# The low part of the queries, taken one group earlier: top-32 attention and a routed feed-forward on one core

## The chip, the cores and the metric

The kernel runs on one core of a Trainium2 chip. The metric is the device time of one launch in microseconds (us); smaller is better. Five engines work side by side: PE multiplies matrices, DVE (VectorE) does the top-32 search, ACT (ScalarE) copies out of PSUM and takes exponentials, POOL (GpSimd) does elementwise side work, SP issues most transfers. Each engine works through its own instructions strictly in the order in which they were written.

## The reference, cut to what matters

```python
# 4 batches, 8 heads, 576 rows, head size 64
scores = q @ k.T / 8
kth = the 32nd largest of each row of scores
attn = softmax(where(scores >= kth, scores, -1e9))
x = attn @ v                       # heads side by side: 2304 tokens x 512
e = argmax(x @ w_gate + bias)      # one of 8 experts for each token
x = gate * (relu(x @ w1[e]) @ w2[e])
h = x @ w_in;  g = 0 below -1, (h + 1)^2 / 4 up to 1, h above
out = g @ w_out
```

The change touches the first stage alone. There the scores are wanted to about the exactness of f32, so q and k are each split into a high part, rounded to a shorter format, and a low part, the rest; three products (high x high, high x low, low x high) make the score.

## The kernel before

**Units and groups.** Heads go in pairs: 16 pairs `j`. One unit is 128 query rows against 576 keys; a pair has 9 units (8 with split products, the ninth, `u == 8`, from the unsplit tiles), so there are 144 units. Two units make a group `g`, 72 groups in all, and one pass of the loop in `attention` handles one group; a pair takes four and a half of them.

**One pass.** In pass `g` the engines are given, in this order: `topk(g)` for DVE (with POOL's part); the masks `w` of group g-1 (ACT, L295); the product with v of group g-2 (PE, L323); half of the scores of group g+4 (PE `qk`, L194 to L196; ACT `sevac`, L204); the turned probabilities of group g-1 (PE, L304 and L306; ACT L311); the first two entries of the list `bg`; the exponentials `e` of group g (ACT, L290); the other half of the scores of g+4; and the rest of `bg`. `bg` is `later[g]`, a list of side steps that `at(g, step, ...)` appends to in order.

**Even and odd passes of DVE.** `topk(g)` takes the eight largest of `lit2` (L251), of `lit` (L253) and of both together (L255), and then four rounds of replacing and searching (L267, L270). An odd pass has, behind L255, also the fold of the next *two* groups: `big`, `c` and `lit2` (L212, L213, L214). So odd passes are long and even ones short.

**What POOL does in a pass.** Two tiny copies of the group before (L240, `edge` and `top`); the factor `nm` (L256), once L255 is done; then `less(g + 1)`, two passes over 128x576 (L227, L233) that make the tile `lit` which DVE's L253 reads in the *next* pass. In an odd pass the first of the two also waits for the fold's end (L214; `add_manual_dep`, "shared port"). Behind these stand the side steps of `bg`: `krest` (the low part of the keys, L179, 128x576), `qrest` (the low part of the queries, L183, 128x512), and `xout` (the normalised output: two short steps on DVE, L344 and L345, then on POOL one product over 128x512, L348, and two over 64x64, L353).

**Where the side steps stand.** For each pair `prep(j, g)` is called with an odd `g`, a few passes before its first scores are due. `turn` transposes the keys or queries on PE (five transposes, L167) and copies them out twice on ACT: `kT` and `kh`, or `qT` and `qh` (L170, L175, L172). `xout` of an older pair is put at the head of the list of an odd pass, and it falls on the same odd passes as `qrest` for all but the first pairs.

Of the kernel before, what the change touches and what calls it, by code (L numbers as in the profile page):

```python
# [65 lines left out]
class Kernel:  # L66
# [32 lines left out]
    def attention(self, moe):  # L99
        nc, tc = self.nc, self.tc  # L100
        with ExitStack() as ctx:
# [264 lines left out]
            def at(g, f, *a):  # L366
                later.setdefault(max(g, 0), []).append((f, a))

            def odd(g):
                return g if g % 2 else g - 1  # L370

            def prep(j, g, *eng):

                at(g - 2, turn, j, "k")
                at(g - 2, krest, j, *eng)
                at(g - 1, turn, j, "q")
                at(g, qrest, j, *eng)

            load(0, nc.scalar)
            load_v(0, vtile(0))  # L380
            load(1)
            load_v(1, vtile(1))
            prep(0, 0, nc.vector)
            for g in range(4):
                for f, a in later.pop(g, []):
# [5 lines left out]
            for j in range(1, len(pairs)):  # L391
                g = odd((9 * j + 1) // 2 - AHEAD - 2)
                prep(j, g)
                if j + 1 < len(pairs):
                    at(g - 2, load, j + 1)
# [1328 lines left out]
```

## Time and profile before

| what | us |
|---|---|
| median of three runs | 1181.84 (1181.74 to 1182.97) |
| profiled execution, its own time | 1180.52 |
| its span in the trace | 1178.9 |
| busy: PE | 1109.3 (94%) |
| busy: DVE | 810.2 (69%) |
| busy: ACT | 709.8 (60%) |
| busy: POOL | 556.2 (47%) |

The shares are means over stages with different limits. Attention with the top-32 search takes about the first 490 us, the routing some 50 more, and the two feed-forward networks the rest. The change lies in the first stage alone, so that stage's own shares and waits are what counts. A wait in a row is the idle time of an engine just before an instruction, put down to the instruction that released it.

### The profile page before, as it was taken

How to read it: one execution, taken by the hardware profiler on the slowest of the kernel's cores; microseconds unless marked ns; L12 is line 12 of the kernel's file. 1: busy time of each engine (PE TensorE's matmuls, PEld its weight loads, DVE VectorE, ACT ScalarE, POOL GpSimd, SP SyncE). 2: the span in 40 equal slices, each digit the busy share in tenths (PEclk: the TensorE clock that was granted, in tenths of full speed). 3: DMA queues.
4: the chain of work that ended last, by engine and by line, in shares of the span. 5: the costliest groups of instructions: out<-in, count | busy, mean ns of one | idle time of the engine just before them, and what ended most of it. 6: DMA issues, size and time to landing. Idle time of an engine off the chain costs nothing. (4 is left out here: it accounts for less than half of the span.)

```text
span 1178.9 us, 24601 instructions
## 1 busy us (share of the span) xinstructions
PE 1109.3 (94%) x8900; PEld 944.4 (80%) x8901; DVE 810.2 (69%) x2523; ACT 709.8 (60%) x1262; POOL 556.2 (47%) x662
## 2 busy tenths in 40 slices
PE   8999899999998997887999999899999999999998
PEld 5777787877887885776888787778899999999897
DVE  6999999999999999887568889487332222323222
ACT  5989998999899985744554455254333333333322
POOL 2776777677677767622324455032322223232222
PEclk8989998999999997998999999999999999999999
DMA  4235573021111003366766565231101001010000
GB/s 88 55 114 176 185 233 119 15 45 44 25 27 37 12 13 126 108 205 212 239 198 214 187 224 179 78 130 54 54 1 37 19 1 54 1 55 1 27 1 28
DMA packets 120842, 106.66 MB, mean 90 GB/s; under 512 B 64384, under 2 KB 88960, under 8 KB 120704
## 3 DMA queue, kind: packets, MB, share of 16 engines
q1 hardware_dynamic: 116320, 94.67, 25.9%
q0 software_dynamic: 2880, 9.44, 2.4%
q8 instruction: 73, 1.20, 0.4%
q10 hardware_dynamic: 1504, 0.82, 0.2%
q14 instruction: 65, 0.53, 0.1%
HBM read 70.30 MB, written 34.60 MB: 89 GB/s over the span
## 5 line engine op out<-in xcount | busy, mean ns | idle before, releaser
L1206 POOL TENSOR_TENSOR gl<-g,gh 128x384 fp32r<-128x384 f32 x96 | 97.2, 1012 | 316.5 <-ACT gh L1205 289.5
L1200 ACT ACTIVATE c<-c,half 128x384 f32<-128x384 f32 x96 | 59.2, 617 | 161.9 <-DVE c L1199 157.1
L306 PE MATMUL tp<-nhuge,w 128*128 128x128 bf16 x720 | 137.1, 227 | 20.8 <-ACT w L295 20.5
L304 PE MATMUL tp<-ident,e 128*128 128x128 f32 x720 | 151.4, 297 | 0.5 <-issue 0.5
L1199 DVE TENSOR_SCALAR c<-h 128x384 f32<-128x384 f32 x95 | 52.8, 556 | 142.5 <-PE h L1057 140.1
L1054 PE MATMUL h<-xh,wih 128*128 128x384 f32 x380 | 130.5, 343 | 5.3 <-DVEq L1110 3.0
L1055 PE MATMUL h<-xh,wil 128*128 128x384 f32 x380 | 129.8, 341 | 0.0
L304 PEld LDWEIGHTS tp<-ident,e 128*128 128x128 f32 x720 | 105.4, 146 | 30.1 <-issue 11.2
L270 DVE MAX8 m<-z 128x8 f32<-128x160 f32 x432 | 117.5, 314 | 0.0
L1365 POOL TENSOR_TENSOR w1l<-w1r,w1h 128x512 fp32r<-128x512 f32 x41 | 57.7, 1408 | 124.7 <-ACT w1h L1364 98.4
L227 POOL TENSOR_TENSOR lit<-s 128x576 int32<-128x576 int32 x66 | 93.4, 1415 | 48.4 <-DVE lit L214 48.4
L1065 PE MATMUL y<-woh,gl 128*128 128x512 f32 x288 | 114.4, 397 | 1.5 <-POOL gl L1206 1.5
L1063 PE MATMUL y<-woh,gh 128*128 128x512 f32 x288 | 112.5, 391 | 1.7 <-ACT yo L1236 0.9
L1203 DVE TENSOR_TENSOR g<-c,h 128x384 f32<-128x384 f32 x95 | 52.6, 554 | 89.2 <-ACT c L1200 89.2
L1064 PE MATMUL y<-wol,gh 128*128 128x512 f32 x288 | 113.7, 395 | 0.0
L311 ACT ACTIVATE a<-tp 128x640 f32<-128x640 f32 x144 | 102.0, 708 | 18.9 <-PE tp L306 14.9
L295 ACT ACTIVATE w<-s,m 128x576 bf16<-128x576 f32 x144 | 103.6, 772 | 13.9 <-DVE m L270 13.9
L323 PE MATMUL tp<-v,a 128*64 128x65 f32 x2880 | 104.7, 228 | 2.1 <-issue 2.0
L323 PEld LDWEIGHTS tp<-v,a 128*64 128x64 f32 x2880 | 93.8, 141 | 15.5 <-issue 8.3
L290 ACT ACTIVATE e<-s,nm 128x576 f32<-128x576 f32 x144 | 103.5, 771 | 4.3 <-POOL nm L256 4.2
L306 PEld LDWEIGHTS <-w 128*128 128x128 bf16 x720 | 79.2, 111 | 26.9 <-ACT w L295 26.5
L204 ACT ACTIVATE s<-sp 128x576 f32<-128x576 f32 x144 | 92.8, 648 | 10.7 <-PE sp L196 9.1
(313 smaller groups left out, 2938.6 us busy)
## 6 DMA issues: line engine op xcount, KB each, us to landing
w1r<-in_moe_w_dram SPq DMA_DIRECT2D x56, 256.0 KB
w2r<-in_moe_w_dram SPq DMA_DIRECT2D x56, 256.0 KB
xs_dr<-zero SPq DMA_DIRECT2D x19, 512.0 KB
ys_dr<-zero SPq DMA_DIRECT2D x19, 512.0 KB
cr<-in_moe_w_in_dram SPq DMA_DIRECT2D x16, 512.0 KB
cr<-in_moe_w_out_dram SPq DMA_DIRECT2D x16, 512.0 KB
rows<-xs_dr SPq DMA_DIRECT2D x20, 256.0 KB
ys_dr<-rows SPq DMA_DIRECT2D x17, 256.0 KB
```

Of the source, the lines that this page charges most:

```text
L270: nc.vector.max(m8[:, i, r + 1], z[:, i])
L290: nc.scalar.activation(e, s, AF.Exp, bias=nm, scale=0.125)
L295: nc.scalar.activation(w, s, AF.Relu, bias=t, scale=-1.0)
L304: nc.tensor.matmul(o, e[:, k0:k0 + 128], self.ident, is_transpose=True, start=True, stop=False)
L306: nc.tensor.matmul(o, w[:, k0:k0 + 128], self.nhuge, start=False, stop=True)
L311: nc.scalar.activation(a, p[:, 0:640], AF.Relu)
L323: nc.tensor.matmul(o[HS[i]], a[:, k0:k0 + 64], v_[:, u % 2 if u < 8 else i, kc, :], start=kc == 0, stop=kc == 4)
L1054: nc.tensor.matmul(p, wh[c], xh[:, c, :], start=c == 0, stop=False)
L1055: nc.tensor.matmul(p, wl[c], xh[:, c, :], start=False, stop=False)
L1063: nc.tensor.matmul(y[t], hh[:, o], wh, start=first, stop=False)
L1064: nc.tensor.matmul(y[t], hh[:, o], wl, start=False, stop=False)
L1065: nc.tensor.matmul(y[t], hl[:, o], wh, start=False, stop=last)
```

## The change

Per pair, the queries are turned in the same odd pass `g - 2` as the keys, as the third entry of the list, and no longer at the head of the list of the even pass `g - 1`. The low part of the queries is taken in the even pass `g - 1` and no longer in the odd pass `g`. Nothing is computed otherwise. For pairs 0 and 1 all four steps fall on pass 0 in either kernel.

```diff
             def prep(j, g, *eng):
 
+
                 at(g - 2, turn, j, "k")
                 at(g - 2, krest, j, *eng)
-                at(g - 1, turn, j, "q")
-                at(g, qrest, j, *eng)
+                at(g - 2, turn, j, "q")
+                at(g - 1, qrest, j, *eng)
```

The new empty line raises all later line numbers of the changed kernel by one. On DVE and SP no instruction changes its place.

POOL, from `less` of pass 10 (the first two rows) through pass 11 to the head of pass 12, before (`lit` is made by less, `x` and `xtail` by xout, `ql` by qrest):

```order
L227 TENSOR_TENSOR lit<-s_1004 128x576
L233 TENSOR_TENSOR lit<-lit,big 128x576
L240 COPY edge<-c 128x4
L240 COPY top<-m_1410 128x2
L256 TENSOR_SCALAR nm<-m_1525 128x2
L227 TENSOR_TENSOR lit<-s 128x576
L233 TENSOR_TENSOR lit<-lit,big 128x576
L348 TENSOR_TENSOR x_73<-xr,r 128x4x128
L353 TENSOR_TENSOR xtail_77<-xr,r 64x64 x2
L183 TENSOR_TENSOR ql_116<-qT,qh_115 128x512
L240 COPY edge<-c 128x4
L240 COPY top<-m_1525 128x2
```

The same stretch of POOL in the changed kernel:

```order
L227 TENSOR_TENSOR lit<-s_1013 128x576
L233 TENSOR_TENSOR lit<-lit,big 128x576
L183 TENSOR_TENSOR ql_116<-qT,qh_115 128x512
L240 COPY edge<-c 128x4
L240 COPY top<-m_1419 128x2
L256 TENSOR_SCALAR nm<-m_1526 128x2
L227 TENSOR_TENSOR lit<-s 128x576
L233 TENSOR_TENSOR lit<-lit,big 128x576
L348 TENSOR_TENSOR x_73<-xr,r 128x4x128
L353 TENSOR_TENSOR xtail_77<-xr,r 64x64 x2
L240 COPY edge<-c 128x4
L240 COPY top<-m_1526 128x2
```

The row of `ql` went ahead of one group's copies, `nm`, less and xout: it stands now behind the less of the even pass, and xout is followed at once by the copies of the next group.

ACT, from the end of pass 9 (`kT`, `kh`) into pass 10, before:

```order
L170 ACTIVATE kT<-sp 128x576
L175 ACTIVATE kh<-sp 128x576
L290 ACTIVATE e<-s,nm 128x576 x2
L204 ACTIVATE s<-sp 128x576
L650 ACTIVATE xT<-sp 128x512
L295 ACTIVATE w<-s,m_1276 128x576 x2
L334 ACTIVATE xr<-tp 128x130
L204 ACTIVATE s<-sp 128x576
L311 ACTIVATE a<-tp 128x640 x2
L170 ACTIVATE qT<-sp 128x576
L172 ACTIVATE qh_115<-sp 128x512
L290 ACTIVATE e<-s_1004,nm 128x576 x2
```

The same stretch of ACT in the changed kernel:

```order
L170 ACTIVATE kT<-sp 128x576
L175 ACTIVATE kh<-sp 128x576
L290 ACTIVATE e<-s,nm 128x576 x2
L204 ACTIVATE s<-sp 128x576
L170 ACTIVATE qT<-sp 128x576
L172 ACTIVATE qh_115<-sp 128x512
L651 ACTIVATE xT<-sp 128x512
L295 ACTIVATE w<-s,m_1276 128x576 x2
L334 ACTIVATE xr<-tp 128x130
L204 ACTIVATE s<-sp 128x576
L311 ACTIVATE a<-tp 128x640 x2
L290 ACTIVATE e<-s_1013,nm 128x576 x2
```

The two copies of the turned queries moved from behind the `a` of pass 10 to the end of pass 9, ahead of the masks `w`; PE's five transposes moved the same way, and ahead of the product with v.

## Rows read from the trace of the kernel before

**Rows 1.** The page's first part: busy time, share of the span and instructions of each engine

```profile
PE 1109.3 (94%) x8900; PEld 944.4 (80%) x8901; DVE 810.2 (69%) x2523; ACT 709.8 (60%) x1262; POOL 556.2 (47%) x662
```

**Rows 2.** Windows: stretch, length, busy of PE, PEld, DVE, ACT, POOL, clock, DMA share, GB/s

```profile
60.00:430.00 370.00, 346.63 (x4404) 288.29 (x4401) 350.42 (x1478) 338.14 (x600) 269.73 (x349) 0.97 0.27 81
430.00:490.00 60.00, 48.94 (x601) 39.95 (x599) 57.10 (x256) 41.60 (x76) 41.89 (x74) 0.89 0.32 107
```

**Rows 3.** Waits from 60 to 430 us: who, for whom, us in total, times, longest

```profile
DVE c L253 <- POOL lit L233: 18.1, 13, 1.5
PE tp L306 <- ACT w L295: 14.7, 20, 2.1
ACT w L295 <- DVE m L270: 11.8, 13, 2.2
ACT a L311 <- PE tp L306: 9.5, 20, 1.1
```

**Rows 4.** Timeline of DVE, passes 11 to 13: start us, us, instruction, [idle before <-releaser]

```profile
88.64 1.34 DVE L212 TENSOR_TENSOR big<-s 128x1152 f32<-128x1152 f32 x1
90.01 0.76 DVE L213 TENSOR_TENSOR c<-big 128x576 f32<-128x576 f32 x1
...
95.19 0.80 DVE L253 MAX8 c<-lit 128x8 f32<-128x288 f32 x2
...
99.48 0.50 DVE L251 MAX8 c<-lit 128x8 f32<-128x144 f32 x2
101.39 0.82 DVE L253 MAX8 c<-lit 128x8 f32<-128x288 f32 x2 [1.41 <-POOL lit L233]
```

**Rows 5.** Timeline of POOL, pass 12

```profile
96.04 0.65 POOL L353 TENSOR_TENSOR xtail<-xr,r 64x64 f32<-64x64 f32 x2
96.77 1.28 POOL L183 TENSOR_TENSOR ql<-qT,qh 128x512 fp32r<-128x512 f32 x1
98.00 0.18 POOL L240 COPY edge<-c 128x4 f32<-128x4 f32 x1
...
99.94 1.42 POOL L233 TENSOR_TENSOR lit<-lit,big 128x576 int32<-128x576 int32 x1
```

**Rows 6.** Timeline of POOL, from the less of pass 10 to the less of pass 11

```profile
85.76 1.41 POOL L233 TENSOR_TENSOR lit<-lit,big 128x576 int32<-128x576 int32 x1
...
88.81 1.24 POOL L256 TENSOR_SCALAR nm<-m 128x2 f32<-128x2 f32 x1 [1.38 <-DVE m L255]
91.53 1.41 POOL L227 TENSOR_TENSOR lit<-s 128x576 int32<-128x576 int32 x1 [1.47 <-DVE lit L214]
93.01 1.42 POOL L233 TENSOR_TENSOR lit<-lit,big 128x576 int32<-128x576 int32 x1
```

**Rows 7.** Timeline of ACT, end of pass 9 and pass 10

```profile
82.47 0.65 ACT L204 ACTIVATE s<-sp 128x576 f32<-128x576 f32 x1
...
86.91 0.65 ACT L170 ACTIVATE qT<-sp 128x576 f32<-128x576 f32 x1
87.46 0.59 ACT L172 ACTIVATE qh<-sp 128x512 fp32r<-128x512 f32 x1
```

**Rows 8.** The tile rq: duration in ns, least/median/most, of PE's transposes of the queries

```profile
L167 PE MATMUL sp<-ident,rq x80: 272/273/421, 6.7 to 408.9; 128*128 128x128 f32 x64, 64*128 64x64 f32 x16
```

**Rows 9.** Timeline of DVE, pass 0: the second step of a fold, halved in size

```profile
18.78 0.74 DVE L212 TENSOR_TENSOR big<-s 128x576 f32<-128x576 f32 x1
19.56 1.54 DVE L213 TENSOR_TENSOR c<-big 128x288 f32<-128x288 f32 x1
```

**Rows 10.** Timeline of POOL, pass 0: the low part of the keys beside that fold

```profile
18.88 1.90 POOL L179 TENSOR_TENSOR kl<-kT,kh 128x576 fp32r<-128x576 f32 x1 [2.81 <-ACT kh L175]
```

**Rows 11.** Timeline of DVE, pass 65: the fold's first step

```profile
440.18 1.34 DVE L212 TENSOR_TENSOR big<-s 128x1152 f32<-128x1152 f32 x1
```

**Rows 12.** Timeline of POOL, pass 65: xout's last products and the copies beside that fold

```profile
439.99 1.69 POOL L353 TENSOR_TENSOR xtail<-xr,r 64x64 f32<-64x64 f32 x2
441.74 0.63 POOL L240 COPY edge<-c 128x4 f32<-128x4 f32 x1
```

**Rows 13.** Windows around the end of pass 27, columns as in Rows 2

```profile
194.00:198.00 4.00, 3.02 (x26) 2.34 (x23) 3.97 (x17) 3.80 (x7) 2.38 (x3) 1.00 0.00 0
198.00:202.00 4.00, 3.33 (x46) 3.09 (x47) 4.00 (x21) 2.92 (x7) 3.87 (x6) 0.71 0.00 1
202.00:206.00 4.00, 4.00 (x25) 3.09 (x24) 4.00 (x16) 1.42 (x3) 2.53 (x5) 0.50 0.32 73
```

## The prediction

> **What bounds the kernel now.** I read the page's shares first [rows 1]: PE 94%, DVE 69%, but these are means over a search stage and two feed-forward stages. The change lies in the first, so the windows come next [rows 2]. From 60 to 430 us, DVE is busy 350.4 of 370 us, PE 346.6, ACT 338.1, POOL 269.7. All but POOL are near full, so who waits for whom decides. The waits of that stretch [rows 3] say it: DVE waits for one thing alone, 13 times, 18.1 us in all, each time L253 for the tile `lit` that POOL's less makes. That is nearly all of its 19.6 idle us. ACT waits for DVE's thresholds (`w` for `m`) 11.8 us, PE for ACT's `w` 14.7 us: these two are released by DVE. So DVE sets the pace, and what holds DVE is POOL.
>
> The timelines show one of the 13. In pass 13 DVE ends L251 at about 99.98 and L253 starts at 101.39, 1.41 us late [rows 4]. POOL finished less at 101.36 [rows 5]. Why so late? In pass 12 POOL first ended xout (`xtail` until 96.69), then took `ql` from 96.77 for 1.28 us, and only at 98.00 came to the copies, behind which `nm` and less stand. A pass with xout but without `ql` would have begun the copies at about 96.7. The 13 waits are those passes in which xout and `ql` stand together (pairs 3 to 15); before them `ql` has no xout in front.
>
> **What is taken away.** `ql` leaves the place between `xtail` and the copies. What goes from the queue is 98.00 - 96.77 = 1.23 us, or 98.00 - 96.69 = 1.31 us with the gap in front of it [rows 5]. I take the middle, 1.27. The wait shown is 1.41, so some 0.14 us stay. 13 x 1.27 = 16.5 us; the bounds are 13 x 1.23 = 16.0 and the whole of the waits, 18.1.
>
> **What is added, and its cover.** `ql` now stands behind the less of an even pass. In pass 10 that less ends at 87.17, and POOL's next deed that anyone waits for, `nm`, started at 88.81 after an idle 1.38 us, since it needs DVE's L255 [rows 6]. There `ql` would run from about 87.12 to 88.40, the two copies from 88.35 (as 98.00 stands to 96.77) to about 88.7, and `nm` at 88.81 as today. Behind `nm` POOL idles another 1.47 us until the fold ends at 91.5, so `nm` may even slip by a us without moving less. Less ends at 94.43 [rows 6] and is read at 95.19 [rows 4]: 0.76 us to spare. I cost the new place at nothing. If the cover is gone, the rivals below give the price.
>
> The margin is thin at one point: `ql` would end at 88.40 and DVE's fold starts at 88.64 [rows 4], 0.24 us later; the last copy may still be running then. Pass 65 shows such a meeting: `xtail` was running when the fold came at 440.18 [rows 12], and the fold took 1.34 us [rows 11] as it does alone [rows 4], while POOL's second product and the copies were held up (1.69 us instead of 0.65 [rows 5], 0.63 instead of 0.18). So small POOL work that meets the fold costs DVE 0 there, and I take 0; the other end is a whole copy, 0.18 us, 13 x 0.18 = 2.3 us.
> The Trainium skill (SBUF — State Buffer, section "Who interferes with whom") says that a DVE instruction with two SBUF inputs and a GpSimd instruction that reads SBUF share an interface, and that whoever issues first holds it while the other fully blocks. By that the fold of pass 65 should have waited for the product ahead of it; no such time is in its row, so the trace does not bear the rule out for something this short. By the rule the sum would be up to those 2.3 us smaller, by the row it stays.
>
> **What is moved on ACT and PE.** Nothing is added, the two ACT copies (0.65 and 0.59 us [rows 7]) and five transposes (5 x 0.273 = 1.4 us [rows 8]) only come earlier, behind the score copy that ends at 83.12 [rows 7]. Even if the transposes lie wholly in front, `qh` is there at 83.12 + 1.4 + 1.2 = 85.7 us, 1.4 us before POOL wants it at 87.12. Queued behind them are the masks `w`, the product with v and the next scores, up to 2.6 us later in the odd pass and as much sooner in the even one. The scores whose copy ends at 83.12 are read by the fold at 88.64, 5.5 us later; that lead is the cover. SP and DVE are not rearranged.
>
> **Does PE keep up?** The stretch shrinks from 370 to 353.5 us. ACT's 338.1 us would be 96% of it, PE's 346.6 us 98%. That is tight, but the clock gives something back. Its mean there is 0.97 [rows 2], which is 0.03 x 370 = 11 us of PE at full clock. Where it falls, PE had been idle shortly before: at the end of pass 27 PE is busy 3.02 and 3.33 of 4 us, and then the clock reads 0.71 and 0.50 [rows 13], down to its lower level of 1.2 GHz. The idle time comes from DVE's late thresholds, so with DVE sooner, fewer such falls are to come.
>
> **The sum.** The profiled execution took 1180.52 us (span 1178.9 and 1.6 around it), the median is 1181.84; the difference is within what the runs scatter. 1180.5 - 16.5 = 1164.0 for the profiled one, 1181.8 - 16.5 = 1165.3 for the median. From 430 us on nothing is rearranged, and DVE is the busiest engine until 490 us (57.1 of 60 us [rows 2]), so the gain should reach the end.
>
> **The rivals.**
> *PE and ACT become the bound.* They can come nearer to DVE only by what they wait for it now: 11.8 us [rows 3]. The rest of the 16.5 would then turn into DVE waiting for scores. For it: 98% of PE, and ACT's 9.5 us of waiting for PE, which don't go. Against: the 5.5 us of lead, the clock, and the idle time after 430 us (PE 11 of 60 us, ACT 18) in which a lag is made good. It gives 1181.8 - 11.8 = 1170.0.
> *The wait becomes a collision.* If `ql` is late by more than its 0.24 us of margin, it meets the fold with a long instruction. Pass 0 shows the price: L213 at half its size, some 0.38 us by half of 0.76 [rows 4], took 1.54 [rows 9] beside the low part of the keys [rows 10], so DVE lost 1.16 us. In the 13 passes, and in pass 3, which had no wait to lose, that is 14 x 1.16 = 16.2 us, the whole gain: 1181.5, no change. It needs `qh` 1.7 us later than worked out above.
> *Slower: POOL's queue stands still.* If `qh` comes later still, POOL waits with `ql` in front of the copies, `nm` and less. `ql` at time T makes less start at T + 1.28 + 0.5 (two copies and `nm`) and end 2.9 us later, so `lit` is late for 95.19 by T - 90.5. From T = 91.8 on that exceeds the 1.27 saved, and each us beyond costs 13 us: 1195 for one. `qh` would have to come 6 us later than worked out; today it ends at 88.05 from its place one pass later [rows 7]. That the change doesn't do what it says is out: the rows of POOL show the move.
>
> **How the numbers follow.** Forecast 1165.3 us with a chance of 0.73; PE and ACT as the bound (1170.0) 0.15; collision (1181.5) 0.06; slower (1195) 0.04; smaller sizes of the latter two, still a gain, 0.02. Below, the range takes in all 18.1 us of waits and 3 us for a fall of the clock that may go in a later stage: 1160.7. Above, it takes 1170.0 and the 2.3 us of the copies: 1172.3. A measurement tells 0.2%, 2.4 us, from no change. Faster: 0.73 + 0.15 + 0.02 and a part of the collision, 0.91; same 0.05; slower 0.04.
>
> **What would show it.** L253's waits for `lit` in the stretch to 430 us should be some 0.1 us each and at most 2 us in all; `ql` should start about 1.3 us before `nm` in odd passes, with the steps of the fold still at 1.34 and 0.76 us; the two passes 12 and 13 should be 1.3 us shorter; the clock's mean should rise above 0.97. The forecast is wrong if new waits of the fold for ACT's `s` appear, if fold steps last over 1 us, or if less of the odd passes ends after L253 wants it.

## The result, and the profile after

The changed kernel takes 1168.24 us (median of four runs, 1167.4 to 1178.4) against 1182.4 before: a ratio of 0.9895 with a 95% interval of 0.9859 to 0.9932, 14.2 us faster. The longest of the four runs had a mean granted clock of 0.965, the others 0.973 to 0.980. 1165.3 was forecast, 16.5 us faster, with 1160.7 to 1172.3 as the range. Taken again later, beside other runs of the kernel before, the same kernel gave 0.9876 (0.9856 to 0.9897) and 0.9930 (0.9907 to 0.9952), that is 14.6 and 9.4 us faster.

The page's first part, as in [rows 1]:

```profile
PE 1105.3 (95%) x8900; PEld 944.2 (81%) x8901; DVE 811.5 (70%) x2523; ACT 708.8 (61%) x1262; POOL 557.7 (48%) x662
```

The windows of the search stage and its end, columns as in [rows 2]:

```profile
60.00:420.00 360.00, 339.34 (x4403) 284.51 (x4404) 353.23 (x1492) 335.00 (x596) 272.33 (x351) 0.99 0.28 85
420.00:480.00 60.00, 51.88 (x633) 42.84 (x632) 57.05 (x256) 44.69 (x81) 42.47 (x74) 0.86 0.33 107
```

DVE is now busy 98% of the stretch and not 95%, PE 94%, ACT 93%, and the clock's mean is 0.99 where it was 0.97. The waits of the stretch from 60 to 430 us, as in [rows 3]:

```profile
ACT a L311 <- PE tp L306: 7.2, 22, 0.9
ACT w L295 <- DVE m L270: 5.9, 6, 1.7
PE sp L167 <- ACT kh L175: 5.6, 12, 0.5
PE tp L306 <- ACT w L295: 5.5, 6, 1.5
...
DVE c L253 <- POOL lit L233: 4.7, 10, 1.4
```

DVE's waits for `lit` fell from 18.1 to 4.7 us. (The view lists waits of more than 0.15 us alone; with the shorter ones it is 5.3 us.) PE and ACT wait for DVE half as long as before or less: they have become the ones that lag. One row is new: twelve times PE waits for `kh` before it turns the queries. It comes up again below. Now the place itself: the timeline of POOL in passes 10 to 12, to be held against [rows 5, 6].

```profile
86.64 1.42 POOL L233 TENSOR_TENSOR lit<-lit,big 128x576 int32<-128x576 int32 x1
88.03 1.28 POOL L183 TENSOR_TENSOR ql<-qT,qh 128x512 fp32r<-128x512 f32 x1
89.26 0.18 POOL L240 COPY edge<-c 128x4 f32<-128x4 f32 x1
89.39 0.18 POOL L240 COPY top<-m 128x2 f32<-128x2 f32 x1
89.69 1.24 POOL L256 TENSOR_SCALAR nm<-m 128x2 f32<-128x2 f32 x1
...
96.92 0.65 POOL L353 TENSOR_TENSOR xtail<-xr,r 64x64 f32<-64x64 f32 x2
97.63 0.19 POOL L240 COPY edge<-c 128x4 f32<-128x4 f32 x1
```

And of DVE in passes 11 to 13, to be held against [rows 4]:

```profile
89.52 1.34 DVE L212 TENSOR_TENSOR big<-s 128x1152 f32<-128x1152 f32 x1
90.89 0.76 DVE L213 TENSOR_TENSOR c<-big 128x576 f32<-128x576 f32 x1
...
101.05 0.82 DVE L253 MAX8 c<-lit 128x8 f32<-128x288 f32 x2 [0.19 <-POOL lit L233]
```

The low part fills POOL's idle time between less and `nm` and ends at 89.31, 0.21 us ahead of the fold; the fold is not longer. Behind `xtail` the copies follow at once, and the wait in pass 13 fell from 1.41 to 0.19 us.

### The profile page after: what moved, and what is told of

Its sections match the earlier page's. It is cut to its first block, busy times and chain, and to the rows that moved or that the text cites. A ratio compares the mean times of both kernels' runs of the same rounds, so it can differ in the third digit from the quotient of the medians.

```text
span 1165.8 us, 24596 instructions
## 1 busy us (share of the span) xinstructions
PE 1105.3 (95%) x8900; PEld 944.2 (81%) x8901; DVE 811.5 (70%) x2523; ACT 708.8 (61%) x1262; POOL 557.7 (48%) x662
## 5 line engine op out<-in xcount | busy, mean ns | idle before, releaser
L304 PE MATMUL tp<-ident,e 128*128 128x128 f32 x720 | 145.6, 293 | 0.0
L306 PE MATMUL tp<-nhuge,w 128*128 128x128 bf16 x720 | 133.4, 224 | 10.1 <-ACT w L295 9.0
L233 POOL TENSOR_TENSOR lit<-lit,big 128x576 int32<-128x576 int32 x66 | 93.3, 1414 | 5.2
```

The lines of the kernel that those rows point to most:

```text
L304: nc.tensor.matmul(o, e[:, k0:k0 + 128], self.ident, is_transpose=True, start=True, stop=False)
L306: nc.tensor.matmul(o, w[:, k0:k0 + 128], self.nhuge, start=False, stop=True)
```

## The experiments

DVE's part of the search stage can be measured apart from the rest: from the start of L251 in pass 0 to its start in pass 64. I read this length, and each wait, from the timeline of every run. "Thirteen" are the waits of the passes that waited before (9, 13, 19, 23, 27, 31, 37, 41, 45, 49, 55, 59, 63), all of them, also those too short for the views; all times are us. The runs were taken in several groups, on different chips, each with its own runs of the kernel before, and that kernel's median went from 1180.5 to 1186.3. So a median is to be held against the one of before beside it. Medians in brackets are of kernels whose later stages do other work. "The change again" is the run after_again, "the change, third" is after_5.

| kernel | median | before, same group | passes 0 to 64 | thirteen | other waits for `lit` (pass) | else |
|---|---|---|---|---|---|---|
| before | 1182.40 | 1182.40 | 419.5 | 18.1 | none | |
| the change | 1168.24 | 1182.40 | 409.0 | 2.1 | 1.42 (29), 1.18 (47), 0.66 (53) | pass 5: +1.9 |
| the change again | 1169.50 | 1184.06 | 404.9 | 2.2 | 1.17 (47) | |
| the change, third | 1174.95 | 1184.39 | 404.8 | 2.1 | 1.17 (47) | |
| turn_only | 1186.03 | 1184.06 | 423.1 | 18.1 | 2.14 (3), 0.28 (29), 2.19 (35) | |
| qrest_only | 1175.66 | 1184.06 | 408.8 | 2.1 | 0.87 (48) | fold steps +4.0 |
| early_k | 1169.00 | 1184.06 | 405.4 | 2.2 | 0.85 (29), 0.63 (53) | |
| k_sooner | 1167.77 | 1186.31 | 406.4 | 2.1 | none | fold waits 2.8 |
| k_sooner_5 | 1168.50 | 1184.39 | 403.6 | 2.2 | none | |
| no_low | 1169.25 | 1186.31 | 403.4 | 2.0 | none | |
| light_before | 1183.68 | 1186.31 | 420.7 | 18.1 | 1.08 (53) | |
| light_after | 1175.25 | 1186.31 | 407.2 | 2.0 | 0.48 (35), 0.66 (47), 0.34 (53) | pass 5: +1.9 |
| act_light | (1291.92) | 1184.39 | 411.3 | 2.2 | 4.44 (29), 0.65 (35), 2.33 (47) | |
| no_logits | (1205.4) | 1180.51 | 404.3 | 2.1 | 1.62 (3) | |

Behind pass 64 nothing is rearranged, but the profiles differ there by several us: 745.3 us before, 742.5, 748.0 and 750.1 for the same changed kernel. That is scatter of the later stages, and it hides a us or two of the search stage in any median.

**The two halves alone.** The edits, against the changed kernel:

```diff
 # turn_only
-                at(g - 1, qrest, j, *eng)
+                at(g, qrest, j, *eng)
 # qrest_only
-                at(g - 2, turn, j, "q")
+                at(g - 1, turn, j, "q")
```

> The queries are turned with the keys, but their low part stays in the odd pass behind xout. Theory (the whole gain is the 1.27 us that the low part leaves out of POOL's queue): DVE's 13 waits for lit stay at 1.3 to 1.5 us, 18 us in all, and the time is that of before, 1182 +- 2. Rival (moving the transposes off the even pass is what helped PE and ACT): 1175 or less, with the 13 waits unchanged.

It gave 1186.03 us, a ratio of 1.0011 (0.9994 to 1.0029). The waits of the stretch from 60 to 430 us:

```profile
DVE c L253 <- POOL lit L233: 20.6, 15, 2.2
```

The thirteen are all there, and the time is 2.0 us above before in its group, so the theory holds: turning the queries sooner gains nothing by itself, and the gain is that of POOL's queue. It even adds waits for `lit` in passes 3 and 35, where the low part of the keys started late because POOL waited for `kh`. The clock was at its lower level ahead of both, from 14 to 31 and from 202 to 212 us; how much of them it explains is open.

> The low part is taken in the even pass, but the queries are still turned in that same even pass, so that qh ends near the 88.05 us of before and not 1.4 us ahead of POOL's need at 87.12. Theory of the collision, as the prediction priced it: the low part starts some 1 us late, meets the fold, one step of the fold takes 1.5 us or more instead of 0.76, 14 x 1.16 = 16.2 us are lost again: 1180 to 1184. Rival (POOL's slack swallows a late low part, the fold is not touched): 1168 as with the whole change.

1175.66 us, 0.9932 (0.9909 to 0.9954), 6.2 us behind the whole change in the same group of runs. Neither theory holds in full. DVE in pass 11:

```profile
88.87 1.34 DVE L212 TENSOR_TENSOR big<-s 128x1152 f32<-128x1152 f32 x1
90.24 1.72 DVE L213 TENSOR_TENSOR c<-big 128x576 f32<-128x576 f32 x1
91.89 0.74 DVE L214 TENSOR_TENSOR lit<-big 128x576 f32<-128x576 f32 x1
```

POOL there:

```profile
89.57 1.78 POOL L183 TENSOR_TENSOR ql<-qT,qh 128x512 fp32r<-128x512 f32 x1 [2.06 <-ACT qh L172]
```

And POOL's waits for the queries from 60 to 415 us:

```profile
POOL ql L183 <- ACT qh L172: 11.2, 5, 5.0
```

The low part came 2.06 us late, met the fold, and L213 took 1.72 instead of 0.76 us. The collision is real and costs 0.96 us here (1.16 was priced), but only where `qh` is late: in passes 3, 11 and 29 the fold got some 1 us longer, in 43 half of that, and over passes 0 to 63 its steps got 4.0 us longer, not 16.2. Turning the queries with the keys is what keeps the low part clear of the fold: that is the worth of the other half.

**No low part at all in the old place.** In the kernel before:

```diff
-                at(g, qrest, j, *eng)
+                if j < 3:
+                    at(g, qrest, j, *eng)
```

> The kernel before, but from pair 3 on the low part of the queries is not taken at all (the tile keeps that of an older pair, so the scores are less exact); all else stands as before. Theory (the new place of the low part costs DVE nothing, only its old place did): the 13 waits fall to 0.1 to 0.3 us as with the change, and the time is that of the change within 2 us. Rival (the new place costs something by the shared port): faster than the change by 3 us or more.

1169.25 us, 0.9865 (0.9839 to 0.9892). From 60 to 420 us:

```profile
DVE c L253 <- POOL lit L233: 1.4, 7, 0.3
```

The thirteen waits fall to 2.0 us, of which the view lists the seven longer ones, and passes 0 to 64 to 403.4, 16.1 us below before. That is the most that taking the low part out of its old place can give. The changed kernel has thirteen waits of the same size, so POOL's work in the new place costs DVE nothing by itself; the rival falls.

**What took the rest.** The changed kernel's passes 0 to 64 are 1.3 to 5.5 us longer than those 403.4. In the first profile three new waits for `lit` hold 3.3 of the 5.5, and pass 5 holds 1.9. ACT, then POOL, then DVE around the start of pass 29:

```profile
195.90 0.64 ACT L175 ACTIVATE kh<-sp 128x576 fp32r<-128x576 f32 x1
```

```profile
196.62 1.41 POOL L179 TENSOR_TENSOR kl<-kT,kh 128x576 fp32r<-128x576 f32 x1 [1.89 <-ACT kh L175]
...
199.91 1.42 POOL L233 TENSOR_TENSOR lit<-lit,big 128x576 int32<-128x576 int32 x1
201.28 1.29 POOL L183 TENSOR_TENSOR ql<-qT,qh 128x512 fp32r<-128x512 f32 x1
202.49 0.20 POOL L240 COPY edge<-c 128x4 f32<-128x4 f32 x1
202.62 1.33 POOL L240 COPY top<-m 128x2 f32<-128x2 f32 x1
```

```profile
201.36 0.82 DVE L253 MAX8 c<-lit 128x8 f32<-128x288 f32 x2 [1.42 <-POOL lit L233]
202.10 0.54 DVE L255 MAX8 m<-c 128x8 f32<-128x160 f32 x2
202.55 1.35 DVE L212 TENSOR_TENSOR big<-s 128x1152 f32<-128x1152 f32 x1
```

`kh` ended at 196.54. POOL waited for it with the low part of the *keys*, 1.89 us, and the less behind it was late for L253. Before, that low part never waited in this stretch. So ACT's copies of the keys did not follow DVE there.

DVE's lead is only a part of the reason. In no_low DVE is just as fast and the queries are turned in their old place. POOL's waits for the keys from 60 to 420 us, first in no_low, then in the change again:

```profile
POOL kl L179 <- ACT kh L175: 0.2, 1, 0.2
```

```profile
POOL kl L179 <- ACT kh L175: 2.0, 2, 1.6
```

In qrest_only, too, it is 0.2 us. The other half of the change has a price, then: the queries' transposes stand close behind those of the keys in the same pass, both write to the two buffers of `sp`, and PE waits until ACT's `kh` has freed one, the new row of 5.6 us in the result. Neither the kernel before nor no_low nor qrest_only has that row; turn_only has it, and late keys, though DVE is no faster there than before. From 155 to 200 us, at a mean clock of 1.00 in both, PE was busy 41.90 us in no_low and 40.57 in the change again, and ACT's masks of group 27 started 1.8 us behind DVE's thresholds in the one and 3.7 in the other. That the new row is what makes this difference fits all these figures; no run took it away alone.

Four runs asked how far the late keys go. In early_k, the keys are turned ahead of the turned probabilities in their pass; in k_sooner, a pass sooner:

```diff
 # early_k, behind the first half of the scores
+                for i, (f, a) in enumerate(bg):
+                    if f is turn and a[1] == "k":
+                        f(*a)
+                        bg[i] = (lambda: None, ())
 # k_sooner (kT and kh in three buffers instead of two)
-                at(g - 2, turn, j, "k")
+                at(g - 3 if j > 2 else g - 2, turn, j, "k")
```

> The whole change, and in its pass the keys are turned ahead of the turned probabilities (PE) and their copies (ACT), some 2.5 us sooner. Theory (three new waits for lit in passes 29, 47 and 53, 3.3 us, come from the keys' low part starting 1.1 to 1.9 us into the even pass because kh was late): these waits go and the time is 1165 +- 1. Rival (PE and ACT are the bound and give the time wherever the keys stand): the wait moves to another place and the time stays 1168 +- 1.

1169.0 us, 0.9874 (0.9855 to 0.9893), as the change in the same group (0.9876). The wait of pass 47 went, those of passes 29 and 53 stayed with 0.85 and 0.63 us. The theory missed its time: a place ahead of the turned probabilities and their copies is not enough. PE's row of waits for `kh` is gone here, so it is not the whole reason either.

> The whole change, and from pair 3 on the keys are turned one pass sooner (three buffers instead of two for kT and kh); their low part stays in its pass. Theory (what is left of the waits for lit, beyond 0.1 to 0.3 us in each of 13 passes, comes from POOL waiting for a late kh): POOL never waits for kh, the waits of passes 29, 47 and 53 go, 2.1 us are left until pass 63, and the time falls by 1 to 3 us below that of the change. Rival (PE and ACT are the bound): the same time, and new waits of the low part of the queries for qh, or of the fold for scores.

1167.77 us, 0.9854 (0.9831 to 0.9878). DVE's waits from 60 to 420 us:

```profile
DVE big L212 <- ACT s L204: 2.8, 1, 2.8
DVE c L253 <- POOL lit L233: 1.5, 7, 0.3
```

The new one of them, in DVE's timeline:

```profile
326.41 1.36 DVE L212 TENSOR_TENSOR big<-s 128x1152 f32<-128x1152 f32 x1 [2.84 <-ACT s L204]
```

Both were right in part. POOL never waits for `kh`, and the waits for `lit` are down to the thirteen small ones. But in this run the fold waited 2.8 us for scores in pass 49 instead: PE and ACT lagged there by all of their lead. The mean clock was 0.83 from 305 to 325 us, just before. It was taken again, beside the change:

> The changed kernel in five rounds, beside the next one: 14 to 15 us faster than before, with one to three waits for lit of 0.6 to 1.4 us beside the thirteen small ones. If pass 5 takes 10.7 and not 8.8 us again, that is one of two ways it can go in any of these kernels.

> The keys turned one pass sooner, again, on the same chip as the change. If the wait of the fold for scores (2.8 us in pass 49) that stood in the place of the waits for kh was bad luck with a fall of the clock, it is gone and the time is 1 to 3 us below the change's; if PE and ACT are the bound, a wait of the fold stands somewhere again and the two are equal within 1 us.

The fold's wait was not there again, the clock from 305 to 325 us was 1.00, DVE's part took 403.6 us, and the kernel 1168.5 us, 0.9869 (0.9855 to 0.9883), while the change took 1174.95, 0.9930 (0.9907 to 0.9952), 9.4 us less than before and not the 14 to 15 expected. In that group k_sooner_5 is 6.5 us below the change, but the search stage holds only 1.2 us of that in the profiles (404.8 against 403.6). The change's six runs went from 1171.2 to 1181.5; the two shortest had a granted clock of 0.979 and 0.977, the others 0.971 to 0.975. What lowered it, and whether it is all of the difference, stays open. Over all groups the change gave medians of 1168.2 to 1175.0 and k_sooner of 1167.8 and 1168.5.

**What makes PE and ACT lag.** Four kernels take work away from them. Without one product (L195) in both kernels:

```diff
-                        nc.tensor.matmul(o, qh[h, q_], kl[h, k_], start=False, stop=False)
```

> The kernel before without the product of the queries' high part with the keys' low part (L195), 64 us less of PE work in the stretch from 60 to 430 us; the scores are that much less exact. Theory (DVE and POOL set the pace of this stage before the change): the 13 waits for lit stay at 1.3 to 1.5 us, 18 us in all, and the time is within 3 us of before. Rival (PE was a bound already): 10 us or more faster.

1183.68 us, 0.9983 (0.9967 to 0.9999), 2.6 us below before in its group, thirteen waits of 18.1 us: DVE and POOL set the pace before, as the theory has it.

> The changed kernel without the same product. Theory (the part of the forecast gain that did not come was lost because PE and ACT could not follow DVE everywhere, so that kh came late): with PE relieved, no wait for lit over 0.3 us is left, DVE's stage ends 15 to 16 us sooner than in the light kernel before, and the difference of the two light kernels is 16 +- 1.5 us. Rival (PE has nothing to do with it): the same waits in passes 29, 47 or 53, and a difference of 14.

1175.25 us, 0.9908 (0.9879 to 0.9936): 8.4 us less than light_before, neither 16 nor 14. DVE's part is 13.5 us shorter, 15.4 without the 1.9 us of pass 5 (light_before's own wait of 1.08 us in pass 53 makes this difference larger); the other 5 to 7 us were lost behind pass 64, where both should do the same, and I can't say why. Three waits of 0.3 to 0.7 us stayed: less work on PE made them smaller, but they did not go.

```diff
 # act_light (`a` is one of four tiles cleared at the start; these lines are left out)
-                nc.scalar.activation(a, p[:, 0:640], AF.Relu)
+                nc.scalar.activation(a[:, 0:320], p[:, 0:320], AF.Relu)
```

> The changed kernel, but ACT copies only the first half of the turned probabilities (320 of 640 columns, L311), some 50 us of ACT's work less over the search stage; the other half stays zero, so the attention output leaves keys out. Theory (kh comes late because ACT, nearly full, lags behind DVE at some pairs): no wait for lit over 0.3 us before pass 64, POOL never waits for kh, DVE's first 63 passes are as short as without any low part (394 us). Rival (PE is what lags): waits of 0.3 to 1.4 us stay in one to three passes.

The routing and thus the later stages differ, so only the search stage counts. Its waits from 60 to 420 us (this kernel's lines are numbered three higher):

```profile
DVE c L256 <- POOL lit L236: 8.9, 10, 4.4
```

And POOL's, from 60 to 415 us:

```profile
POOL kl L182 <- ACT kh L178: 8.8, 3, 4.9
```

Worse, not better: the theory did not hold. It is not refuted either, for the edit disturbed something else. From 155 to 200 us, where these keys fell behind, the mean clock was 0.89 in this run and 1.00 in the change again, so PE was slower just there. What ACT's load alone does stays open.

> The changed kernel as it is, for the scatter of its profile. If the 1.9 us that DVE lost in pass 5, where its small copies met POOL's iotas, come from the change, they are there again; if they are a chance of arbitration, pass 5 takes 8.8 us as before in this profile or the other kernels' of this group. Time 1168 +- 1.

Pass 5 took 8.8 us in that run, so the 1.9 us do not come from the change. The run has no fall of the clock from 35 to 390 us, and still the wait of 1.17 us in pass 47; so a slow clock was not needed for that one. What is common to the late passes is their place: passes 27 and 45, in which the keys come late, stand right behind or at the end of the routing logits of a batch (`gate_logits`, one 128-row piece in each of four or five passes, with entries in the lists of passes 23 to 26 and 41 to 45 here, and with a hand-over from PE to ACT). From group 23 to group 27 of that run, ACT's masks fall back from 0.7 to 3.7 us behind DVE, and to 5.5 us in group 28. The last run left the logits out:

```diff
 # no_logits (a line that clears the logits at the start is left out)
-                            for c in range(len(self.x_tiles(b))):
-                                at(g + 4 + c, self.gate_logits, b, c)
```

> The changed kernel without the routing logits of the first three batches (side steps on PE and ACT, five passes at a time behind each fourth pair; the logits are zero, so the routing and all later stages differ and only the search stage is to be read). Theory (PE and ACT fall behind DVE in just those passes, and kh of the next pairs is late for it): no wait for lit beyond the thirteen small ones, passes 0 to 64 take 403.5 us, as without any low part. Rival (the lag is of PE and ACT as a whole, wherever it comes to light): waits of 0.3 to 1.4 us in one to three passes stay.

From 60 to 420 us (lines one higher):

```profile
DVE c L254 <- POOL lit L234: 1.5, 7, 0.3
```

No late keys in passes 29, 47 or 53, and ACT's masks of group 27 are 0.6 us behind DVE. Passes 0 to 64 took 404.3 us with a wait of 1.62 in pass 3, 402.7 without it. So the logits' passes are where PE and ACT fall behind. For pass 47 the comparison is firm, though it rests on one profile: all three of the change have that wait. Pass 29 waited in one of the three and pass 53, which does not stand behind a batch's logits, in one; one profile without them shows little. PE's new waits for `kh` are in this run too, 5.6 us, so by themselves they do not make the keys late; no_low has the logits without these waits, and hardly late keys. Both together seem to be needed.

## Why the prediction was right, and where it was too high

**What bounds the kernel** was right: the thirteen waits were POOL's, they went, and no_low, turn_only and light_before each confirm it from another side. Passes 12 and 13 together became 1.2 us shorter in the trace; 1.3 was said.

**What is taken away** was forecast as 16.5 us and is 16.1: the thirteen waits fell from 18.1 to 2.1 us. In each pass 0.09 to 0.28 us stayed, 0.14 was said. But the sign "at most 2 us in all" was missed, at 4.7 us by the same view, and what lies above it is the late keys.

**The new place at no cost** held. The low part ran from 88.03 to 89.31, against an end 0.24 us ahead of the fold as forecast and 0.21 as measured. In pass 29, where it was late, only the tiny copies met the fold: `top` took 1.33 us instead of 0.18, L212 1.35 instead of 1.34, as in [rows 11, 12].

**Does PE keep up**, and with it **what is moved on ACT and PE**, is the step that was incomplete. I had looked for a lag at `qh` (1.4 us ahead of need) and at the fold's scores (5.5 us of lead). It came to light at a third place, whose order the change does not touch: `kh`, wanted by POOL at the very start of an even pass, whose less has 0.3 us to spare (87.17 by [rows 6] for the L253 of about 87.5) and not the 0.76 that I had worked out for odd passes. This cost 1.2 us in two profiles of the change and 3.3 in another. And "nothing is added" on PE overlooked that the two turnings, now in one pass, share the two buffers of `sp`: PE waits 5.6 us for `kh`, which had been put at nothing. The rival "PE and ACT become the bound" had the lag, though it let DVE wait for scores, which only k_sooner showed; its 1170.0 is nearer to 1168.24 than the forecast is.

**The clock** did rise, from 0.97 to 0.99 [rows 2]: between 60 and 430 us the trace has it at its lower level in five stretches before and in three with the change. That the falls which went had followed DVE's waits is argued, not shown.

**The first profile's own 13.1 us** (1180.52 to 1167.4) are a sum of parts, of which only the first was foreseen: 16.1 from the thirteen, less 3.3 for late keys and 1.9 in pass 5, and 2.8 back behind pass 64, which is within that part's scatter; 0.6 more are spread over small differences. That the median came within 3 us of the forecast is in part luck: the same kernel gained 14.2, 14.6 and 9.4 us in three groups of runs.

**The collision** was priced at 1.16 us and 14 passes; qrest_only shows 0.96, and only where the queries are late. In the change no fold of passes 1 to 63 is longer for it.

## What to carry to other kernels

When an engine is the bound by its waits for a helper, look at the helper's queue and at where its idle time stands: 1.28 us of work moved from a full pass into a pass with a 1.4 us gap removed 16 us. Then ask of every engine that feeds the helper whether it can follow the faster one, and check the spare time of *each* hand-over and not only of those that the edit moves; here it was the keys, left in their place, that came late. Look in the new trace for waits that were not there before: here PE's for a buffer that two steps, now close together, share. A side step that comes in bursts (the logits of a batch) shows up as lag only once the others have no waits left to hide it.

## What the runs showed of the hardware

Pass 5 went in two ways. DVE's copy and `tensor_scalar`, beside small POOL iotas and the low part of the keys, took 1.13 and 1.41 us in the first profile of the change, and 0.41 and 0.41 in its second. The first profile, DVE and then POOL's low part of the keys:

```profile
55.66 1.13 DVE L688 COPY b<-bias 128x144 f32<-128x144 f32 x1
...
57.04 1.41 DVE L701 TENSOR_SCALAR lt<-i 128x64 f32<-128x64 f32 x1
```

```profile
56.90 1.50 POOL L179 TENSOR_TENSOR kl<-kT,kh 128x576 fp32r<-128x576 f32 x1
```

The second:

```profile
56.13 0.41 DVE L688 COPY b<-bias 128x144 f32<-128x144 f32 x1
...
56.81 0.41 DVE L701 TENSOR_SCALAR lt<-i 128x64 f32<-128x64 f32 x1
```

```profile
57.37 1.42 POOL L179 TENSOR_TENSOR kl<-kT,kh 128x576 fp32r<-128x576 f32 x1
```

The pass takes 8.8 us in twelve of the fourteen profiles and 10.7 in two, the change's first and light_after. The order of instructions is the same in the change and its repetition, so it is the two engines' relative timing that decides; the Trainium skill (SBUF — State Buffer, section "Who interferes with whom") says that copies and `tensor_scalar`, in modes that use two ports, can contend with GpSimd for a shared pair of ports and that whoever issues first holds it. For `tensor_scalar` the trace agrees: in the first profile it started behind the low part of the keys and ended with it, in the second it had ended, at 57.22, before that began. The copy met POOL's iotas in both profiles and was held in one alone, so for it the rule does not tell which way it goes.

The same section's full blocking agrees with qrest_only: L213 stood 0.96 us longer while the low part ran. For the copy `edge`, under way when the fold's first step came in pass 29 of the change, the step shows 0.01 us; there the measurement decides.
